# Decoding the first twelve weight blocks by way of PSUM, with their low parts made on GpSimd, in a fused attention and feed-forward kernel

## The chip, the cores and the metric

The kernel runs on one core of a Trainium2 chip. The metric is device time in microseconds (us) for one execution. In the profile PE is the matrix engine (PEld its weight loads), DVE is VectorE, ACT is ScalarE, POOL is GpSimd and SP is SyncE, which here only issues DMAs.

## The reference

A sliding-window attention with four sink tokens feeds a feed-forward block. There are 4 batches, 8 heads, 768 positions and a head size of 64. The feed-forward matrices arrive as 64-bit floats.

```python
scores = (q @ k.transpose(0, 1, 3, 2)) / np.sqrt(D)
keep = is_sink | ((rel >= 0) & (rel < window))       # n_sink = 4, window = 128
a = softmax(np.where(keep, scores, -1e9))
x = (a @ v).transpose(0, 2, 1, 3).reshape(3072, 512)
h = x @ w_in                                          # 512 x 2048
g = np.where(h >= 1, h, np.where(h <= -1, 0, (h + 1) ** 2 / 4))
out = g @ w_out                                       # 2048 x 512
```

## The kernel before

**The attention** is cut into 64 units of one batch, one head and 384 query rows. Units 0 to 15 take a short path (`NATIVE = 16`). A unit's scores are three PE steps (L239). For each, DVE adds the mask, takes the row's peak and moves the tile out of PSUM (L243), and ACT takes the exponential (L246). POOL adds a small constant to the three row sums (L251), DVE takes their reciprocals (L252), and one DVE row (L266) and two ACT rows (L264) scale the probabilities. PE transposes them (L324, L326), ACT copies them back (L327, L331), and PE multiplies them with the values (L367). ACT copies two heads' result to `xn` (L369). For every fourth part of the model dimension, ACT and DVE split `xn` into a high and a low part (L479, L480). Eight units make one chunk of 384 tokens; the program has eight chunks, called chunk 0 to 7 here.

**The feed-forward part** works on one chunk at a time, beside the attention of the next one. `stage1` (L439) multiplies into `h_ps`, ACT and DVE apply g and split it (L446 to L450; in the first chunk POOL makes the low part, L450), and `stage2` (L458) multiplies into `o_ps`, three PSUM banks of the pool `ps_o`.

**The weights** are 32 blocks of 128 x 512 numbers, 16 of `w_in` and 16 of `w_out` in turn (n = 0 to 31), each 512 KB of 64-bit floats. `weights(n)` issues the load of block n+3 at the latest (L167; blocks 0 to 7 on SP's queue, the others on ACT's) and decodes block n with `decode`. Three DVE instructions put a 32-bit float together out of the two 32-bit words: a shift with a mask (L153), the sign and top bits (L154), the low word's bits (L155). ACT rounds that to the matrix format, which is the high part (L156), and DVE subtracts it, which gives the low part (L157). The three results share one tile `o` of the pool `moe`, which has two buffers.

**The order.** PE's order is written out by hand: `spread` lays one list of steps evenly between those of another. The order on the other engines comes from a scheduler that places each instruction where it expects it to be ready. Blocks of weights can therefore stand earlier in DVE's row than their step. The lists are cut by two constants: the first `WFIRST` weight steps are spread over the attention of chunk 0, those up to `WMID` over the first half of chunk 0's feed-forward part, which runs beside the attention of chunk 1, and the last four over the next stage:

```python
prev = wsteps[:WFIRST]
        if c == 0:
            prev = spread(wsteps[WFIRST:WMID], moe_steps(rows[0], tail, x0, range(NJ0), part))
        elif c == 1:
            prev = spread(wsteps[WMID:], moe_steps(rows[1], tail), WLEAD)
```

Of the kernel before, what the change touches and what calls it, by code (L numbers as in the profile page):

```python
# [8 lines left out]
F32 = mybir.dt.float32  # L9
F32R = mybir.dt.float32r  # L10
I32 = mybir.dt.int32
U8 = mybir.dt.uint8
AF = mybir.ActivationFunctionType
ALU = mybir.AluOpType

B, H, S, D = 4, 8, 768, 64
DM, DFF = 512, 2048
P = 128
# [15 lines left out]


CHECK = range(34, 34 + 2 * NJ)
WFIRST = 6
WMID = 28
AHEAD = 3
SYNC = 8  # L40
# [12 lines left out]
def attn_ffn(ctx, tc, qk, vx, vs, par, w_in, w_out, out):  # L53
    nc = tc.nc
# [3 lines left out]
    moe = ctx.enter_context(tc.tile_pool(name="moe", bufs=2))  # L58
# [3 lines left out]
    ps_o = ctx.enter_context(tc.tile_pool(name="ps_o", bufs=3, space=bass.MemoryType.PSUM))  # L62
# [12 lines left out]
    low, high = par_f[:, :, 0], par_f[:, :, 1]  # L75
# [66 lines left out]
    w_i = [const.tile([P, 2, DM], F32R, name=f"wi{j}") for j in range(NJ)]  # L142
    w_o = [None] * NJ
# [4 lines left out]
    both = const.tile([P, 2 * P], I32, name="both")  # L148
    nc.gpsimd.memset(both, -1)

    def decode(t, w, words):
        low, x = words[:, :, 0], words[:, :, 1]
        nc.vector.tensor_scalar(w, x, 3, 0x3FFFFFFF, op0=ALU.logical_shift_left, op1=ALU.bitwise_and)  # L153
        nc.vector.scalar_tensor_tensor(w, x, -0x40000000, w, op0=ALU.bitwise_and, op1=ALU.bitwise_or)  # L154
        nc.vector.scalar_tensor_tensor(w, low, 29, w, op0=ALU.logical_shift_right, op1=ALU.bitwise_or)  # L155
        nc.scalar.copy(t[:, 0], w.bitcast(F32))  # L156
        nc.vector.tensor_tensor(t[:, 1], w.bitcast(F32), t[:, 0].bitcast(F32), op=ALU.subtract)  # L157

    top = {}

    def weights(n):
        def f():
            j, i = n // 2, n % 2
            for k in range(n, min(n + min(AHEAD, NJ - n // 2 - 1) + 1, 2 * NJ)):
                if k not in raw:
                    raw[k] = wpool.tile([P, 2 * DM], I32, name="w")
                    (nc.sync if k < SYNC else nc.scalar).dma_start(raw[k], (w_in, w_out)[k % 2][k // 2].bitcast(I32))  # L167
            words = raw[n].rearrange("p (c two) -> p c two", two=2)
            if i:
                w_o[j] = wpool.tile([P, 2, DM], F32R, name="w")  # L170
            decode((w_i, w_o)[i][j], moe.tile([P, DM], I32, name="o"), words)
        return f


# [307 lines left out]
    def moe_steps(row0, tail, x=None, js=range(NJ), part=None):  # L482


        if x is None:
            x = xpool.tile([P, 2, NCT, CT * P], F32R, name="x")
        o_ps, hs = [], {}
        steps = [(0.0, lambda ct=ct: split(x, ct)) for ct in range(NCT)] if js[0] == 0 else []
        second = tail[:]
        for n, j in enumerate(js):  # L490
            if n < LAG:
                steps += second[n * CT:(n + 1) * CT]
            steps += [(0.49, lambda j=j, ct=ct: stage1(x, j, ct, hs, row0)) for ct in range(NCT)]
            if n >= LAG:
                steps += [(0.65, lambda j=js[n - LAG], tt=tt: stage2(o_ps, hs, j, tt, row0, js, part)) for tt in range(CT)]
        tail[:] = [(0.65, lambda j=j, tt=tt: stage2(o_ps, hs, j, tt, row0, js, part)) for j in js[-LAG:]
                   for tt in range(CT)]
        return steps

    def spread(a, b, lead=1.0):  # L500

        wa, wb = (sum(w for w, _ in s) for s in (a, b))
        steps, n, da, db = [], 0, 0.0, 0.0
        for step in b:
            while n < len(a) and da * lead * wb <= db * wa:
                steps.append(a[n])
                da += a[n][0]
                n += 1
            steps.append(step)
            db += step[0]  # L510
        return steps + a[n:]
# [7 lines left out]
    rows = [b * S + t0 * P for b, t0 in chunks]  # L519
    prev = wsteps[:WFIRST]  # L520
    n0 = 0
    tail = []
    for c in range(len(chunks)):
# [5 lines left out]
# [3 lines that stand above are left out]
# [24 lines left out]
    ps = ps_a.tile([P, 512], F32, name="ps_a")  # L556
# [56 lines left out]
    with tc.If(other_v > 0):  # L613
        with tc.tile_pool(name="gen", bufs=1) as gen:

            for n in range(2 * NJ):
                words = gen.tile([P, DM, 2], I32, name="words")
                nc.sync.dma_start(words.rearrange("p c two -> p (c two)"), (w_in, w_out)[n % 2][n // 2].bitcast(I32))
                xf = words[:, :, 1].bitcast(F32)
                m = gen.tile([P, DM], F32, name="m")  # L620
                nc.vector.tensor_tensor(m, xf, xf, op=ALU.mult)
                nc.vector.scalar_tensor_tensor(xf, m, TINY2, xf, op0=ALU.is_ge, op1=ALU.mult)
                decode((w_i, w_o)[n % 2][n // 2], m.bitcast(I32), words)
            for t0 in (0, CT):
                keep = gen.tile([P, CT, S], F32, name="keep")
                kidx = gen.tile([P, S], I32, name="kidx")
                r = gen.tile([P, S], F32, name="r")
                for i in range(CT):
                    m = keep[:, i]
                    nc.gpsimd.iota(kidx, pattern=[[-1, S]], base=(t0 + i) * P, channel_multiplier=1)  # L630
                    nc.vector.tensor_copy(r, kidx)
                    nc.vector.tensor_scalar(m, r, w_f, None, op0=ALU.is_lt)
                    nc.vector.scalar_tensor_tensor(m, r, 0.0, m, op0=ALU.is_ge, op1=ALU.mult)
                    nc.gpsimd.iota(kidx, pattern=[[1, S]], base=0, channel_multiplier=0)
                    nc.vector.tensor_copy(r, kidx)
                    nc.vector.scalar_tensor_tensor(m, r, n_f, m, op0=ALU.is_lt, op1=ALU.max)
                    nc.vector.tensor_scalar(m, m, 0.125, None, op0=ALU.mult)
                for b in range(B):
                    for h in range(H):
                        general(gen, keep, b, h, t0)  # L640
                    tail = []
                    for _, f in moe_steps(b * S + t0 * P, tail) + tail:
                        f()
# [37 lines left out]
```

## Time and profile before

| what | value |
|---|---|
| median of 3 runs | 736.66 us (735.27 to 738.84) |
| the profiled execution | 737.31 us, span of its instructions 735.5 us |
| PE busy | 696.8 us, 95% of the span |
| DVE busy | 528.7 us, 72% |
| ACT busy | 507.0 us, 69% |
| POOL busy | 307.2 us, 42% |
| DMA | 77.79 MB, mean 106 GB/s |

The span is the time from the first to the last instruction of the program; about 1.8 us of the profiled execution lie outside it. A share over the whole span says little here: the first 100 us, in which the weights are decoded, look different from the rest, so the stages are read one by one.

### The profile page before, as it was taken

What the parts mean: (1) busy time and instruction counts of PE and PEld (TensorE: products, weight loads), DVE (VectorE), ACT (ScalarE), POOL (GpSimd) and SP (SyncE); (2) the same over time, 40 slices, a digit from 0 to 9 for tenths busy, and PEclk for the clock granted to TensorE, in tenths of its full rate; (3) what the DMA queues carried; (4) which work ended last, traced back from release to release, by engine and by line L of the source; (5) the groups of instructions that cost most, each with busy time, mean ns of one, the idle gap of its engine ahead of it and who ended that gap; (6) DMA issues with size and microseconds to landing.
All of it is one profiled execution on the core that took longest, in us unless ns stands there. A gap on an engine that the chain in (4) does not pass through costs nothing.

```text
span 735.5 us, 12356 instructions
## 1 busy us (share of the span) xinstructions
PE 696.8 (95%) x3841; PEld 615.7 (84%) x3841; DVE 528.7 (72%) x1396; ACT 507.0 (69%) x1313; POOL 307.2 (42%) x537
## 2 busy tenths in 40 slices
PE   5669889899999999999999999999999999999996
PEld 3337678789999999999979998899889999989995
DVE  8999996987655666568777887877887777742221
ACT  4888797776576665578767876778767776645342
POOL 3112166554346434236554555645666454500000
PEclk9989999999999999999999999999999999999998
DMA  8987543312131311134423542324334342101001
GB/s 268 327 268 255 170 115 96 99 46 54 42 100 45 100 40 58 34 119 128 124 81 117 156 121 85 116 73 156 124 114 119 103 131 85 66 2 44 0 1 47
DMA packets 48265, 77.79 MB, mean 106 GB/s; under 512 B 13632, under 2 KB 32064, under 8 KB 48192
## 3 DMA queue, kind: packets, MB, share of 16 engines
q1 hardware_dynamic: 44736, 64.34, 28.9%
q10 hardware_dynamic: 3456, 12.58, 4.8%
q8 instruction: 32, 0.52, 0.3%
q14 instruction: 41, 0.34, 0.2%
HBM read 69.83 MB, written 7.08 MB: 105 GB/s over the span
## 4 chain that ended last, share of the span: by engine, by line
PE 64%; DVE 17%; ACT 7%; DMA 7%; issue 2%; POOL 2%; SPq 0%; ACTq 0%; POOLq 0%; DVEq 0%
PE o_ps L458 28%; PE h_ps L439 27%; PE ps_a L402 4%; DMA w<-w_in 4%; PE ps_a L239 3%; ACT p L246 2%; DVE p L266 2%; DVE k_s L223 1%; DVE o L154 1%; PE ps_a L334 1%; DVE o L155 1%; DVE p L258 1%; DVE gl L450 1%; DVE p L243 1%; DVE o L153 1%
## 5 line engine op out<-in xcount | busy, mean ns | idle before, releaser
L439 PE MATMUL h_ps<-x,wi 128*128 128x384 f32 x1536 | 308.7, 340 | 0.4 <-DVE x L480 0.4
L439 PEld LDWEIGHTS h_ps<-x,wi 128*128 128x128 f32 x1536 | 263.5, 188 | 9.3 <-DVE x L480 0.7
L458 PE MATMUL o_ps<-w,gh 128*128 128x512 f32 x768 | 244.6, 399 | 0.0
L458 PE MATMUL o_ps<-w,gl 128*128 128x512 f32 x384 | 151.3, 394 | 0.0
L458 PEld LDWEIGHTS o_ps<-w,gh 128*128 128x128 f32 x768 | 135.2, 189 | 15.7 <-issue 0.3
L446 ACT ACTIVATE g<-h_ps,half 128x384 f32<-128x384 f32 x128 | 73.9, 578 | 69.7 <-PE h_ps L439 67.7
L448 DVE SCALAR_TENSOR_TENSOR g<-g,h_ps 128x384 f32<-128x384 f32 x128 | 70.2, 549 | 68.6 <-ACT g L447 68.0
L246 ACT ACTIVATE p<-p,peak 128x260 f32<-128x260 f32 (+1 forms) x192 | 93.9, 489 | 33.9 <-DVE peak L243 32.0
L225 POOL TENSOR_TENSOR q_l<-r,q_h 128x384 fp32r<-128x384 f32 x48 | 50.3, 1047 | 142.5 <-ACT q_h L224 141.6
L449 ACT CAST gh<-g 128x384 fp32r<-128x384 f32 x128 | 65.5, 512 | 56.9 <-DVE g L448 55.9
L243 DVE CUSTOM_DVE_ANT_0 p<-ps_a,m 128x260 f32<-128x260 f32 (+1 forms) x176 | 68.5, 398 | 31.8 <-PE ps_a L239 30.5
L239 PE MATMUL ps_a<-k_s,q_h 128*128 128x260 f32 (+1 forms) x240 | 71.2, 345 | 18.6 <-DMA k_s<-qk 6.1
L458 PEld LDWEIGHTS o_ps<-w,gl 128*128 128x128 f32 x384 | 72.3, 188 | 17.5
L450 DVE TENSOR_TENSOR gl<-g,gh 128x384 fp32r<-128x384 f32 x112 | 68.0, 607 | 24.5 <-ACT gh L449 23.6
L223 DVE TENSOR_TENSOR k_s<-k_r,k_s 64x524 fp32r<-64x524 f32 (+1 forms) x44 | 45.4, 1032 | 40.9 <-ACT k_s L221 40.9
L239 PEld LDWEIGHTS ps_a<-k_s,q_h 128*128 128x128 f32 x240 | 45.2, 203 | 33.3 <-issue 10.9
L447 ACT ACTIVATE g<-g 128x384 f32<-128x384 f32 x128 | 67.0, 523 | 2.7
L346 POOL TENSOR_SCALAR_AFFINE_SELECT pt<-pt 128x384 fp32r<-128x384 f32 (+1 forms) x96 | 50.8, 530 | 24.2 <-DVE pt L339 21.7
L266 DVE TENSOR_SCALAR p<-p,stat 128x132 f32<-128x132 f32 (+1 forms) x160 | 59.1, 418 | 0.3
L344 POOL TENSOR_SCALAR_AFFINE_SELECT pt<-pt 128x384 fp32r<-128x384 f32 (+1 forms) x96 | 52.5, 547 | 8.9 <-ACT pt L338 3.9
L251 POOL TENSOR_SCALAR stat<-stat 128x3 f32<-128x3 f32 x64 | 28.6, 447 | 62.2 <-ACT p L246 53.8
L402 PEld LDWEIGHTS ps_a<-pt,v_s 128*128 128x128 f32 x304 | 46.5, 189 | 2.0
(117 smaller groups left out, 955.3 us busy)
## 6 DMA issues: line engine op xcount, KB each, us to landing
r<-qk SPq DMA_DIRECT2D x48, 192.0 KB
k_r<-qk SPq DMA_DIRECT2D x32, 262.0 KB
again<-w_in SPq DMA_DIRECT2D x16, 512.0 KB
again<-w_out SPq DMA_DIRECT2D x16, 512.0 KB
w<-w_in ACTq DMA_DIRECT2D x12, 512.0 KB
w<-w_out ACTq DMA_DIRECT2D x12, 512.0 KB
out<-o SPq DMA_DIRECT2D x23, 256.0 KB
r<-vx SPq DMA_DIRECT2D x32, 128.0 KB
```

The source lines that it names most:

```text
L239: nc.tensor.matmul(ps[:, lo:260], lhsT=q[:, i * P:(i + 1) * P], rhs=k_s[:, c0:c0 + 260 - lo], start=(j == 0), stop=(j == len(qs) - 1))
L243: nc.vector.tensor_tensor_reduce(out=p[:, i, lo:260], in0=ps[:, lo:260], in1=m, scale=-0.0625 if units.index(u) < NATIVE else -0.125, scal ...
L246: nc.scalar.activation(p[:, i, lo:260], p[:, i, lo:260], AF.Exp, bias=peak_i, scale=-1.0, accum_out=stat[:, i:i + 1])
L266: (nc.gpsimd if eng == "p" else nc.vector).tensor_scalar(p[:, i, lo:260], p[:, i, lo:260], r, None, op0=ALU.mult)
L402: nc.tensor.matmul(z, lhsT=w, rhs=y, start=(n == 0), stop=(n == len(mms) - 1))
L439: nc.tensor.matmul(h_ps[:, :T], lhsT=w_i[j][:, w, ct * P:(ct + 1) * P], rhs=x[:, y, ct], start=(ct == 0 and n == 0), stop=(ct == NCT - 1 a ...
L446: nc.scalar.activation(g, h_ps[:, :T], AF.Relu, bias=half, scale=0.5)
L447: nc.scalar.activation(g, g, AF.Square)
L448: nc.vector.scalar_tensor_tensor(g, g, 1.0, h_ps[:, :T], op0=ALU.min, op1=ALU.max)
L449: nc.scalar.copy(gh, g)
L450: (nc.gpsimd if row0 == GL_POOL else nc.vector).tensor_tensor(gl, g, gh.bitcast(F32), op=ALU.subtract)
L458: nc.tensor.matmul(o_ps[tt], lhsT=gg[:, tt * P:(tt + 1) * P], rhs=w_o[j][:, w], start=(j == js[0] and n == 0), stop=(j == js[-1] and n == 2))
```

## The change

`WFIRST` goes from 6 to 12. For these first 12 blocks `decode` gets a PSUM tile of the pool `ps_o`. The first two DVE instructions write to it and the second and third read from it, so that each of the three has one SBUF tensor as input, the words, and from the second on one PSUM tensor. The third still writes `o` in SBUF. The low part of these blocks is subtracted by GpSimd instead of DVE. The other 20 blocks are decoded as before, and so is the copy in the branch at the end, which doesn't run with these inputs.

```diff
-WFIRST = 6
+WFIRST = 12
...
-    def decode(t, w, words):
+    def decode(t, w, words, ps=None):
         low, x = words[:, :, 0], words[:, :, 1]
-        nc.vector.tensor_scalar(w, x, 3, 0x3FFFFFFF, op0=ALU.logical_shift_left, op1=ALU.bitwise_and)
-        nc.vector.scalar_tensor_tensor(w, x, -0x40000000, w, op0=ALU.bitwise_and, op1=ALU.bitwise_or)
-        nc.vector.scalar_tensor_tensor(w, low, 29, w, op0=ALU.logical_shift_right, op1=ALU.bitwise_or)
+        y = w if ps is None else ps
+        nc.vector.tensor_scalar(y, x, 3, 0x3FFFFFFF, op0=ALU.logical_shift_left, op1=ALU.bitwise_and)
+        nc.vector.scalar_tensor_tensor(y, x, -0x40000000, y, op0=ALU.bitwise_and, op1=ALU.bitwise_or)
+        nc.vector.scalar_tensor_tensor(w, low, 29, y, op0=ALU.logical_shift_right, op1=ALU.bitwise_or)
         nc.scalar.copy(t[:, 0], w.bitcast(F32))
-        nc.vector.tensor_tensor(t[:, 1], w.bitcast(F32), t[:, 0].bitcast(F32), op=ALU.subtract)
+        (nc.vector if ps is None else nc.gpsimd).tensor_tensor(t[:, 1], w.bitcast(F32), t[:, 0].bitcast(F32), op=ALU.subtract)
...
-            decode((w_i, w_o)[i][j], moe.tile([P, DM], I32, name="o"), words)
+            decode((w_i, w_o)[i][j], moe.tile([P, DM], I32, name="o"), words,
+                   ps_o.tile([P, DM], F32, name="o_ps").bitcast(I32) if n < WFIRST else None)
```

In the changed file the lines of `decode` stand 3 lower (L153 to L157 become L156 to L160) and all that follows `weights` 4 lower (L243 becomes L247, L252 becomes L256, L266 becomes L270). The text below uses the numbers of before for both.

DVE's row of before, from the last rows of unit 3's scores (`m_106` is the mask of a unit's third part, `m_109` of its first) to the first part of unit 4's:

```order
L243 ISA p,peak<-ps_a,m_106 128x260
L243 ISA peak 128x1
L155 SCALAR_TENSOR_TENSOR o<-w,o 128x512
L153 TENSOR_SCALAR o<-w 128x512
L154 SCALAR_TENSOR_TENSOR o<-w,o 128x512
L252 RECIPROCAL stat<-stat 128x3
L155 SCALAR_TENSOR_TENSOR o<-w,o 128x512
L266 TENSOR_SCALAR p<-p,stat 128x128
L243 ISA p,peak<-ps_a,m_109 128x128
```

The same place in DVE's row of the change, from unit 3's reciprocals to the first part of unit 4's scores:

```order
L256 RECIPROCAL stat<-stat 128x3
L157 SCALAR_TENSOR_TENSOR o_ps<-w,o_ps 128x512
L270 TENSOR_SCALAR p<-p,stat 128x128
L156 TENSOR_SCALAR o_ps<-w 128x512
L158 SCALAR_TENSOR_TENSOR o<-w,o_ps 128x512
L157 SCALAR_TENSOR_TENSOR o_ps<-w,o_ps 128x512
L156 TENSOR_SCALAR o_ps<-w 128x512
L158 SCALAR_TENSOR_TENSOR o<-w,o_ps 128x512
L157 SCALAR_TENSOR_TENSOR o_ps<-w,o_ps 128x512
L158 SCALAR_TENSOR_TENSOR o<-w,o_ps 128x512
L247 ISA p,peak<-ps_a,m_109 128x128
```

More of the decoding now stands ahead of unit 4's scores: by then nine rows of L155 have gone by against six, and seven rows of decoding lie between unit 3's reciprocals and unit 4's scores against one.

POOL's row of before, from the constants at the start (`wi_151` is the `w_in` part of block 0, `wi_152` of block 2 and so on; `w` is a `w_out` part) over the first units' row sums:

```order
L113 MEMSET m1n 128x4
L251 TENSOR_SCALAR stat<-stat 128x3 x3
L298 TENSOR_TENSOR vsx_137<-vs_r,vsx_137 44x64
L251 TENSOR_SCALAR stat<-stat 128x3
L283 MEMSET v_s 128x128
```

The same place in POOL's row of the change:

```order
L113 MEMSET m1n 128x4
L255 TENSOR_SCALAR stat<-stat 128x3 x2
L160 TENSOR_TENSOR wi_151<-o,wi_151 128x512
L160 TENSOR_TENSOR w<-o,w 128x512
L160 TENSOR_TENSOR wi_152<-o,wi_152 128x512
L160 TENSOR_TENSOR w<-o,w 128x512
L255 TENSOR_SCALAR stat<-stat 128x3
L302 TENSOR_TENSOR vsx_137<-vs_r,vsx_137 44x64
L160 TENSOR_TENSOR wi_153<-o,wi_153 128x512
L255 TENSOR_SCALAR stat<-stat 128x3
```

Four low parts now stand ahead of the row sum of unit 2, and a fifth ahead of that of unit 3.

## Rows read from the trace of the kernel before

**Rows 1.** The page: busy tenths of PE and DVE in 40 slices.

```profile
PE   5669889899999999999999999999999999999996
...
DVE  8999996987655666568777887877887777742221
```

**Rows 2.** Stretches: length, then busy PE, PEld, DVE, ACT, POOL, clock, DMA, GB/s.

```profile
20.00:40.00 20.00, 13.53 (x78) 7.65 (x76) 19.44 (x61) 17.50 (x56) 2.28 (x8) 0.96 0.92 315
...
60.00:80.00 20.00, 19.39 (x115) 16.06 (x113) 19.93 (x52) 17.39 (x50) 5.43 (x7) 1.00 0.64 198
...
82.30:105.80 23.50, 21.83 (x126) 17.40 (x126) 22.41 (x53) 19.28 (x55) 9.78 (x11) 0.93 0.49 151
```

**Rows 3.** Timeline of DVE at 27 us: start, duration, instruction, [idle before it].

```profile
26.72 0.42 DVE L243 CUSTOM_DVE_ANT_0 p<-ps_a,m 128x260 f32<-128x260 f32 x1
...
27.06 0.42 DVE L153 TENSOR_SCALAR o<-w 128x512 int32<-128x512 int32 x1
27.40 0.54 DVE L480 TENSOR_TENSOR x<-xn,x 128x384 fp32r<-128x384 f32 x1
27.87 0.68 DVE L157 TENSOR_TENSOR w<-o,w 128x512 fp32r<-128x512 f32 x1
28.47 0.68 DVE L154 SCALAR_TENSOR_TENSOR o<-w,o 128x512 int32<-128x512 int32 x1
29.08 0.28 DVE L243 CUSTOM_DVE_ANT_0 p<-ps_a,m 128x128 f32<-128x128 f32 x1
29.28 0.08 DVE L243 DVE_READ_ACCUMULATOR2_ANT peak<- 128x1 f32 x1
```

**Rows 4.** Timeline of DVE at the reciprocals of unit 12.

```profile
80.65 0.16 DVE L252 RECIPROCAL stat<-stat 128x3 f32<-128x3 f32 x1
```

**Rows 5.** Timelines of ACT and PE behind it.

```profile
81.76 0.91 ACT L264 ACTIVATE p<-p,stat 128x260 f32<-128x260 f32 x2
...
82.33 0.86 PE L324 MATMUL ps_a<-ident,p 128*128 128x128 f32 x2 [2.38 <-ACT p L264]
```

**Rows 6.** PE's waits from 82.3 to 160 us: total us, times, longest.

```profile
PE ps_a L324 <- ACT p L264: 2.7, 2, 2.4
PE ps_a L239 <- DVE sk L341: 2.7, 2, 1.7
PE ps_a L239 <- DVE peak L243: 1.2, 2, 0.8
PE ps_a L239 <- ACT xn L369: 1.1, 1, 1.1
```

**Rows 7.** Timeline of POOL: tensor-tensor rows of 384 and of 192 elements.

```profile
69.13 1.00 POOL L450 TENSOR_TENSOR gl<-g,gh 128x384 fp32r<-128x384 f32 x1 [4.84 <-ACT gh L449]
...
72.24 1.50 POOL L450 TENSOR_TENSOR gl<-g,gh 128x384 fp32r<-128x384 f32 x1 [0.75 <-ACT gh L449]
...
93.72 1.34 POOL L225 TENSOR_TENSOR q_l<-r,q_h 128x384 fp32r<-128x384 f32 x1
...
95.78 1.25 POOL L450 TENSOR_TENSOR gl<-g,gh 128x384 fp32r<-128x384 f32 x1
...
110.06 0.59 POOL L293 TENSOR_TENSOR v_s<-r,v_s 128x192 fp32r<-128x192 f32 x1 [1.17 <-ACT v_s L292]
```

**Rows 8.** Timeline of DVE beside those rows of POOL.

```profile
69.21 1.20 DVE L153 TENSOR_SCALAR o<-w 128x512 int32<-128x512 int32 x1
...
72.79 1.04 DVE L266 TENSOR_SCALAR p<-p,stat 128x128 f32<-128x128 f32 x1
...
94.11 1.50 DVE L155 SCALAR_TENSOR_TENSOR o<-w,o 128x512 int32<-128x512 int32 x1
...
96.17 0.39 DVE L243 CUSTOM_DVE_ANT_0 p<-ps_a,m1n 128x260 f32<-128x260 f32 x1
```

**Rows 9.** DMA queue of ACT (q10: packets, MB, share): whole span.

```profile
q10 hardware_dynamic: 3456, 12.58, 4.8%
```

**Rows 10.** The same queue from 20 to 30 us.

```profile
q10 hardware_dynamic: 349, 1.30, 35.8%
```

## The prediction

> **What bounds the kernel now.** I looked at the slices of the page first. PE is short of work only in the first slices; from 160 us on it is busy in every one, so a microsecond gained or lost before that goes into the end time [rows 1]. The early part is therefore read by stretches. There DVE is full: 19.44 of 20 us from 20 to 40, 19.93 from 60 to 80 [rows 2]. PE has 13.53 us in the first of these, but 19.39 in the second, and 115 matmul rows there, 5.75 in a microsecond. From 82.3 to 105.8 it has 126, at that pace 21.9 of the 23.5 us [rows 2]. So up to some 60 us DVE alone sets the pace, and from there PE has only little room left.
>
> DVE works in order and hardly waits, so a row's time is that of all that stands ahead of it. What one row costs is the step from its start to the next start, not its duration, since neighbours overlap: L153 0.34 us, L157 0.60, L154 0.61 [rows 3]; I use 0.34 for L153 and 0.60 for L154, L155 and L157. A block costs DVE 2.14 us.
>
> The clearest place where PE waits for this queue is at unit 12's end: DVE's reciprocals (L252) start at 80.65, ACT scales the probabilities at 81.76, PE transposes them at 82.33 after 2.38 us of idling [rows 4, 5]. Behind it PE's waits up to 160 us come to 7.7 us, these 2.4 among them, which leaves 5.3, most of it on DVE [rows 6].
>
> **The change part by part.** *The low part leaves DVE:* 12 rows of 0.60, minus 7.2 us there.
>
> *The first instruction writes to PSUM.* No DVE row of before writes there. The lower bound is what it costs now, 0.34 for 512 numbers, the upper bound L154's 0.60 on the same tile. Rows that read PSUM are the nearest: L243 takes 0.34 to the next start for 260 numbers and 0.20 for 128 [rows 3], 1.06 ns a number, which at 512 gives 0.34 + 252 x 1.06 ns = 0.61. I take 0.60: 12 x 0.26 = 3.1 us back. The Trainium skill speaks against this edit at that point: "VectorE: DVE Perf Modes", section "Why PSUM operands drop a tier", says that the double rate of 32-bit tensor-scalar work needs both SBUF ports and that any PSUM operand ends it. By that rule the price is likewise the upper one; if only the row of L153 counted, it would be nothing and the sum 3.1 us less.
>
> The second and third instruction I leave at 0.60, the pace of one number a cycle that L243's slope has too.
>
> *The order.* This is the largest part. I counted the rows of L153, L154, L155 and L157 ahead of three places, in both orders; the attention's rows ahead of them are the same but for a row or two.
> - Chunk 0's last split (the fourth L480), which the feed-forward part needs: before 18, 18, 18, 17, after 22, 21, 21, 8. Before 18 x 0.34 + 53 x 0.60 = 37.9 us; after 12 x 0.60 + 10 x 0.34 + 50 x 0.60 = 40.6. **2.7 us later.**
> - Unit 12's reciprocals: before 23, 23, 23, 21 (48.0 us), after 27, 27, 26, 14 (12 x 0.60 + 15 x 0.34 + 67 x 0.60 = 52.5). **4.5 us later.**
> - The last split of chunk 1 (the eighth L480): 29 of each before (62.1 us), after 29, 29, 29, 17 (58.0). **4.1 us earlier.**
>
> The saving is thus paid out only at the end of the stretch; in its middle, where PE waits, the changed queue is late.
>
> *GpSimd's low parts.* A POOL subtraction takes 1.00 us for 384 numbers undisturbed and 0.59 for 192 [rows 7], so 1.00 + 128 x 2.1 ns = 1.27 for 512, 15.3 us for twelve. POOL is busy for only 2.28 of 20 us there [rows 2], so it has the time. But beside such rows some of DVE's are held up: L153 takes 1.20 instead of 0.42, L266 1.04 where another row of 128 numbers takes 0.28 [rows 3], L155 1.50 instead of 0.68, each ending about when a POOL row does, while L243 at 96.17 with its tensor in PSUM is not touched, 0.39 [rows 7, 8]. A meeting costs up to 0.8 us, 0.4 in the mean. The twelve low parts lie between 14 and 40 us or so, 15.3 of 26 us, a share of 0.59. DVE rows of the kinds held up stand there 13 times by the order: six L266, two L480 and five of blocks 12 and 13. 13 x 0.59 x 0.4 = **3.1 us**, bounds 0 and 13 x 0.8 = 10.4.
>
> *Waits for words and buffers.* The loads from block 8 on stand in ACT's row behind the same roundings as before, while DVE comes to the blocks sooner. The queue moves 3456 packets for 24 blocks, 144 each [rows 9], and 349 between 20 and 30 us [rows 10]: blocks 8 and 9 are there by 30, block 10 not. By my count DVE comes to block 9 at 30.2 (before 35.3), to block 10 at 31.8 (38.5). The margin of about 5 us is used up, hardly overdrawn: **0.5 us**, bounds 0 and 3. The roundings of twelve blocks are ACT's as before (17.50 of 20 us busy [rows 2]). POOL's row sums stand behind low parts now, so DVE's reciprocals may wait for them; that is the third rival.
>
> *What PE gets back.* At unit 12 PE is late by 4.5 + 3.1 + 0.5 = 8.1 us. Behind that it comes later than before while DVE's queue is shorter, so what it waited for is ready: the 5.3 us of waits are taken back. Sum: +2.8 us on the profiled 737.31 (its span of 735.5 and some 1.8 around it), 740.1. That execution lay 0.65 us above the median, so I forecast **739.5 us** against 736.66.
>
> **The rivals.**
> 1. *The end of the stretch decides* (faster). If PE can swallow its backlog, what counts is the third place, 4.1 us earlier. With the port met half as often (1.5) and 0.5 for words, and with 2.0 us fewer hold-ups late in the stretch, since 10 rows of decoding are left there instead of 26: -4.1, so 733.2, 732.5 beside the median. For it speaks that PE's busy time includes matmuls that wait; against it that PE does 5.4 rows a microsecond there, close to its pace of 5.75 [rows 2]. It decides if PE needs under 17 us for that work. If the first instruction also kept 0.34, it would be 3.1 less.
> 2. *The port is met in full* (slower): 13 x 0.59 x 0.8 = 6.1 instead of 3.1, as low parts follow each other without gaps: +5.8, 742.5. The four low parts in a row in POOL's order speak for it.
> 3. *GpSimd paces the decoding* (slower). The tile `o` has two buffers and is now freed by POOL, so block n+2's third instruction waits for the low part of block n, behind ACT's rounding. Rounding and subtraction and some 0.5 us of queueing make 0.6 + 1.27 + 0.5 = 2.4 us; DVE has about 3 us from one use of a buffer to its next, so it fits until ACT comes more than 0.6 us late. ACT is nearly full and waits for DVE's scores itself. At 0.6 us for each of ten blocks: +8.8, 745.5.
>
> **How the numbers follow.** About 0.5%, 3.7 us, is what a measurement of this kernel can tell from no change. Forecast 0.46, with a range of its own from 736 to 742; rival 1 0.20; rival 2 0.16; rival 3 0.18. A tenth of the forecast's case lies above 740.3. So faster 0.20, same 0.42, slower 0.38. The range goes from 732, near rival 1, to 746, near rival 3.
>
> **What would show it.** L156 writing `o_ps` steps on by 0.60, not 0.34. POOL gets twelve rows of about 1.3 us before 45 us, and L266 and L480 of the first units show durations near 1 us. The fourth L480 starts some 3 to 6 us later than before, unit 12's reciprocals 5 to 9 us after 80.65, and PE's wait there grows. From 90 us on PE waits for DVE less. The prediction is wrong if L156 keeps 0.34, if DVE idles in the first 40 us (rival 3), or if PE catches up before 105 us.

## The result and the profile after

The change makes the kernel slower by 0.9%: 743.43 us in the median of 7 runs (741.07 to 744.46) against 736.66 (734.61 to 738.84, 7 runs), a ratio of 1.009 with a 95% interval of 1.0067 to 1.0113. The profiled execution took 743.43 us with a span of 741.7, 6.2 more than before.

Where the time goes is seen by the same instruction in both traces (start in us; lines of the changed file in this table; PE's order is the same in both kernels but for 62 of 3841 places):

| place | before | after | shift | forecast |
|---|---|---|---|---|
| chunk 0's first split (first L484) | 27.40 | 35.92 | +8.5 | |
| its last split (fourth L484) | 62.36 | 68.64 | +6.3 | 2.7 and up to 3.6 for port and words |
| unit 12's reciprocals (L256) | 80.65 | 88.20 | +7.5 | +8.1 |
| sixth block of g in the feed-forward part (L452) | 103.79 | 106.82 | +3.0 | +7.7 |
| tenth block of g | 133.05 | 141.56 | +8.5 | +6.2 |
| 16th to 48th block of g | 163.90 to 319.48 | 172.44 to 328.00 | +8.5 | +2.8 |
| end | 735.5 | 741.7 | +6.2 | +2.8 |

Behind unit 12 the forecast column takes off before's waits of PE as they come: 0.36 us at 97 us, 1.5 at 105 to 108, 3.6 at 137 to 148. So two losses, not one: the forecast one, and one more between 107 and 142 us. The +3.0 at the sixth g is a place in DVE's row; PE's own rows are later there, as is shown further down.

The slices of the page after: PE's are fuller in the third and sixth, emptier in the fourth and eighth, DVE's nearly as full as they were [rows 1], and PE's granted clock dips from the second to the fourth slice and in the eighth.

```profile
PE   5678899799999999999999999999999999999996
...
DVE  8899956797754576658788788878878777842221
...
PEclk9778999899999999999999999999999999999999
```

The stretches [rows 2]: DVE is no longer full from 20 to 40 us (17.68 for 19.44), GpSimd's time rose from 2.28 to 10.52, and PE's clock is 0.68 where it was 0.96. The last row is new.

```profile
20.00:40.00 20.00, 13.11 (x51) 7.60 (x50) 17.68 (x50) 14.56 (x46) 10.52 (x14) 0.68 0.92 318
82.30:105.80 23.50, 21.31 (x129) 17.28 (x129) 18.16 (x50) 20.28 (x61) 8.30 (x12) 1.00 0.43 125
140.00:160.00 20.00, 16.64 (x79) 14.45 (x80) 19.69 (x50) 11.03 (x31) 8.90 (x16) 0.83 0.22 66
```

Before, that last stretch was PE's:

```profile
140.00:160.00 20.00, 18.96 (x108) 16.81 (x108) 17.65 (x48) 14.12 (x40) 10.48 (x18) 1.00 0.24 70
```

DVE's timeline after:

```profile
25.11 0.69 DVE L156 TENSOR_SCALAR o_ps<-w 128x512 int32<-128x512 int32 x1
25.71 0.68 DVE L158 SCALAR_TENSOR_TENSOR o<-w,o_ps 128x512 int32<-128x512 int32 x1
...
40.96 1.24 DVE L270 TENSOR_SCALAR p<-p,stat 128x128 f32<-128x128 f32 x1
42.16 1.48 DVE L156 TENSOR_SCALAR o<-w 128x512 int32<-128x512 int32 x1
...
88.20 0.18 DVE L256 RECIPROCAL stat<-stat 128x3 f32<-128x3 f32 x1
...
135.23 0.43 DVE L156 TENSOR_SCALAR o<-w 128x512 int32<-128x512 int32 x1 [0.59 <-DMA part<-o]
...
139.75 0.43 DVE L156 TENSOR_SCALAR o<-w 128x512 int32<-128x512 int32 x1 [1.35 <-DMA part<-o]
...
141.56 0.55 DVE L452 SCALAR_TENSOR_TENSOR g<-g,h_ps 128x384 f32<-128x384 f32 x1
```

L156 into PSUM steps on by 0.60 (25.11 to 25.71) where L153 took 0.34 [rows 3]. The two rows at 41 and 42 us, written to SBUF, last 1.24 and 1.48 and end 0.08 and 0.28 us after GpSimd's last two low parts:

```profile
40.85 1.27 POOL L160 TENSOR_TENSOR wi<-o,wi 128x512 fp32r<-128x512 f32 x1 [0.21 <-ACT wi L159]
42.09 1.27 POOL L160 TENSOR_TENSOR w<-o,w 128x512 fp32r<-128x512 f32 x1
```

PE's timeline after: the wait at unit 12 shrank from 2.38 [rows 5] to 1.16, one of 1.03 us for the values of a unit is new at 115 us, and one of 3.18 us stands at 142 us.

```profile
89.67 0.73 PE L328 MATMUL ps_a<-ident,p 128*128 128x128 f32 x2 [1.16 <-ACT p L268]
...
114.87 0.64 PE L338 MATMUL ps_a<-ident,p 128*128 128x128 f32 x3 [1.03 <-ACT v_s L296]
...
142.16 1.44 PE L443 MATMUL h_ps<-x,wi 128*128 128x384 f32 x6 [3.18 <-DVE g L452]
...
145.85 0.56 PE L243 MATMUL ps_a<-k_s,q_h 128*128 128x260 f32 x1 [0.86 <-DVE sk L345]
```

The wait at 142 us is followed back to the stores of chunk 0's partial sums. Its feed-forward part is cut in two; at the end of the first half ACT copies three PSUM tiles to tiles `o`, SP stores them to `part`, and the last four weight blocks are decoded next, in the same two buffers of `o`. SP's queue before and after (`x3` with 3.34 us is a group of three):

```profile
125.48 1.15 SPq L465 DMA_DIRECT2D part<-o  x2
...
128.22 0.32 SPq L465 DMA_DIRECT2D part<-o  x1
```

```profile
132.27 3.34 SPq L469 DMA_DIRECT2D part<-o  x3
```

Before, DVE began the first of these blocks at 128.42 without a wait. After, its rows of L156 at 135.23 and 139.75 wait 0.59 and 1.35 us for the stores (rows above), 6.8 and 7.8 us later than before; L452, which PE waits for, stands behind them at 141.56, 8.5 later. Its input from ACT is there at 138.36 (the last row of the ACT timeline below); of the 3.2 us from then on, 1.35 are the second wait for the stores and the rest are rows of DVE ahead of it. Of the 6.8 us, 5 are those by which PE is already late at 125 us. The other 2 us arise at ACT: PE has the ninth block's h ready at 123.52 before and at 128.53 after, and ACT starts its g at 123.56 and at 130.63. Before, the cast of the next unit's values (L292) stood between the copies:

```profile
124.60 0.57 ACT L464 COPY o<-o_ps 128x512 f32<-128x512 f32 x1
125.44 0.35 ACT L292 CAST v_s<-r 128x192 fp32r<-128x192 f32 x1 [0.28 <-DMA r<-vx]
```

After, it stands ahead of that block's g and the copies, and waits for its load:

```profile
130.25 0.35 ACT L296 CAST v_s<-r 128x192 fp32r<-128x192 f32 x1 [1.10 <-DMA r<-vx]
130.63 0.58 ACT L450 ACTIVATE g<-h_ps,half 128x384 f32<-128x384 f32 x1
...
131.68 1.05 ACT L468 COPY o<-o_ps 128x512 f32<-128x512 f32 x2
...
137.82 0.54 ACT L451 ACTIVATE g<-g 128x384 f32<-128x384 f32 x1
```

### The profile page after: what moved, and what is told of

The parts are those of the page before. It is cut to its first block, busy times and chain, and to the rows that moved or that the text cites. A ratio compares the mean times of both kernels' runs of the same rounds, so it can differ in the third digit from the quotient of the medians.

```text
span 741.7 us, 12358 instructions
## 1 busy us (share of the span) xinstructions
PE 702.5 (95%) x3841; PEld 621.0 (84%) x3841; DVE 523.5 (71%) x1384; ACT 507.3 (68%) x1313; POOL 316.5 (43%) x549
## 4 chain that ended last, share of the span: by engine, by line
PE 62%; DVE 16%; ACT 8%; DMA 7%; issue 3%; POOL 2%; SPq 0%; ACTq 0%; POOLq 0%; DVEq 0%
PE o_ps L462 27%; PE h_ps L443 26%; PE ps_a L406 4%; PE ps_a L243 3%; ACT p L250 2%; DMA w<-w_out 2%; DVE p L270 2%; PE ps_a L338 1%; DVE k_s L227 1%; DVE o L158 1%; DVE gl L454 1%; DVE p L247 1%; DMA again<-w_out 1%; DVE p L262 1%; DVE g L452 1%
## 5 line engine op out<-in xcount | busy, mean ns | idle before, releaser
L462 PEld LDWEIGHTS o_ps<-w,gh 128*128 128x128 f32 x768 | 135.4, 189 | 15.8 <-issue 0.3
L452 DVE SCALAR_TENSOR_TENSOR g<-g,h_ps 128x384 f32<-128x384 f32 x128 | 70.2, 549 | 68.9 <-ACT g L451 68.3
L229 POOL TENSOR_TENSOR q_l<-r,q_h 128x384 fp32r<-128x384 f32 x48 | 48.8, 1017 | 151.3 <-ACT q_h L228 143.1
L247 DVE CUSTOM_DVE_ANT_0 p<-ps_a,m 128x260 f32<-128x260 f32 (+1 forms) x176 | 68.3, 399 | 33.1 <-PE ps_a L243 32.0
L243 PE MATMUL ps_a<-k_s,q_h 128*128 128x260 f32 (+1 forms) x240 | 71.4, 347 | 14.1 <-DMA k_s<-qk 5.3
L243 PEld LDWEIGHTS ps_a<-k_s,q_h 128*128 128x128 f32 x240 | 46.0, 208 | 27.3 <-issue 10.8
L270 DVE TENSOR_SCALAR p<-p,stat 128x132 f32<-128x132 f32 (+1 forms) x160 | 58.9, 417 | 0.5
L255 POOL TENSOR_SCALAR stat<-stat 128x3 f32<-128x3 f32 x64 | 26.6, 415 | 53.7 <-ACT p L250 45.0
```

What stands on the lines that cost most here:

```text
L243: nc.tensor.matmul(ps[:, lo:260], lhsT=q[:, i * P:(i + 1) * P], rhs=k_s[:, c0:c0 + 260 - lo], start=(j == 0), stop=(j == len(qs) - 1))
L247: nc.vector.tensor_tensor_reduce(out=p[:, i, lo:260], in0=ps[:, lo:260], in1=m, scale=-0.0625 if units.index(u) < NATIVE else -0.125, scal ...
L270: (nc.gpsimd if eng == "p" else nc.vector).tensor_scalar(p[:, i, lo:260], p[:, i, lo:260], r, None, op0=ALU.mult)
L452: nc.vector.scalar_tensor_tensor(g, g, 1.0, h_ps[:, :T], op0=ALU.min, op1=ALU.max)
L462: nc.tensor.matmul(o_ps[tt], lhsT=gg[:, tt * P:(tt + 1) * P], rhs=w_o[j][:, w], start=(j == js[0] and n == 0), stop=(j == js[-1] and n == 2))
```

## The experiments

A ratio is against runs of the kernel before on the same chip (736.70 us for the first four kernels, 736.72 for the next four, 737.57 and 736.84 for the last two pairs); its 95% interval stands behind it (a ratio can differ from the quotient of the two medians by up to 0.001). Shifts are those of the first table: us later than in the trace of before, each from one profiled execution, which lies up to 2.0 us from its kernel's median (path for 6 blocks 1.9, path for 12 2.0 and before with 5 ahead 2.0 above).

### The parts of the change apart

Before with the order's constant alone:

```diff
-WFIRST = 6
+WFIRST = 12
```

> WFIRST is 12, the decoding is that of before. Theory A (DVE's order is to blame: blocks stand ahead of the scores that PE waits for): by the rows counted in its order, chunk 0's last split is 4.2 us later than before, unit 12's reciprocals 5.9 us later, chunk 1's last split not earlier; with 1 to 3 us of waits for words and little taken back the time is 5 to 9 us above before. Rival B (the new decoding is to blame, by the PSUM price, the port and GpSimd): without it the order costs nothing, within 2 us of before.

The change with all low parts on DVE:

```diff
-        (nc.vector if ps is None else nc.gpsimd).tensor_tensor(t[:, 1], ...)
+        nc.vector.tensor_tensor(t[:, 1], ...)
```

> As the change, but the low parts stay on DVE. Theory A: the counted rows put unit 12's reciprocals 8.4 us after those of before and the last split of chunk 1 3.1 us after, so it is slower than the change: 8 to 13 us above before. Rival B, with GpSimd as the cause (port and the buffers of o): faster than the change, at most 4 us above before.

The change without PSUM, the low parts still on GpSimd:

```diff
-        y = w if ps is None else ps
+        y = w
```

> As the change, but the three decoding rows stay in SBUF. Theory A: the counted rows put unit 12's reciprocals 2.3 us before those of before and chunk 1's last split 7.2 us before; with two SBUF inputs the decoding rows now meet the twelve low parts on GpSimd, which gives back 3 to 8 us up to 45 us, and words cost up to 3: 0 to 7 us above before, below the change. Rival (meetings are as rare as in the change, 2 us): 2 to 4 us below before. Second rival (the PSUM way is what keeps DVE going): slower than the change.

The change with the partial sums stored from ACT's queue, so that they don't stand in SP's:

```diff
-                nc.sync.dma_start(part[tt], o)
+                nc.scalar.dma_start(part[tt], o)
```

> The change, with the partial sums' stores issued by ACT instead of SP. Theory C (of the change's loss, about 5 us arise between 106 and 150 us, where block 30's first decoding row waits for a buffer of o that a store frees, which stands in SP's queue behind loads): 3 to 5 us faster than the change, 738.5 to 740.5. Rival (that wait only shows what DVE and PE owe from before): within 1 us of the change.

| kernel | median us | ratio | fourth split | unit 12 | sixth g | tenth g | end of span |
|---|---|---|---|---|---|---|---|
| the change | 743.43 | 1.009 [1.0067, 1.0113] | +6.3 | +7.5 | +3.0 | +8.5 | +6.2 |
| WFIRST = 12 alone | 740.95 | 1.0059 [1.0037, 1.0081] | +5.3 | +6.7 | +3.4 | +6.1 | +4.0 |
| low parts on DVE | 744.53 | 1.0098 [1.0072, 1.0123] | +5.8 | +7.8 | +5.3 | +9.2 | +7.4 |
| no PSUM | 746.10 | 1.0126 [1.01, 1.0152] | +10.5 | +10.6 | +8.3 | +11.1 | +8.7 |
| stores on ACT's queue | 742.50 | 1.0071 [1.0046, 1.0097] | +5.4 | +6.6 | +2.1 | +5.0 | +5.9 |

The order alone costs 4.3 us of the 6.8 (theory A said 5 to 9) and makes most of the lateness at the fourth split and at unit 12. Taking twelve subtractions from DVE is worth 1.1 us in the end, less than the two intervals can tell. Moving the stores off SP's queue changed little: the tenth g came earlier, but by the 16th the shift was +7.6 again, so the theory that SP's queue is at fault fell. In that trace DVE waits for the stores for 0.81 us instead of 1.94, and PE waits less at the tenth g (0.84) but for 2.63 us at 143.30 and 1.80 at 154.51, both for DVE.

Without PSUM the kernel is the slowest of the four, as the second rival said (theory A had it faster than the change), and its trace says why. Rows of DVE from 9 to 60 us (busy us, mean ns), first without PSUM, then the change:

```profile
L158 DVE SCALAR_TENSOR_TENSOR o<-w,o 128x512 int32<-128x512 int32 x16 | 14.5, 907 | 0.1
L157 DVE SCALAR_TENSOR_TENSOR o<-w,o 128x512 int32<-128x512 int32 x16 | 13.8, 860 | 0.2
```

```profile
L156 DVE TENSOR_SCALAR o_ps<-w 128x512 int32<-128x512 int32 x12 | 8.3, 688 | 3.0 <-DMA w<-w_out 2.2 <-DMA w<-w_in 0.8
L157 DVE SCALAR_TENSOR_TENSOR o_ps<-w,o_ps 128x512 int32<-128x512 int32 x12 | 8.2, 683 | 0.0
L158 DVE SCALAR_TENSOR_TENSOR o<-w,o_ps 128x512 int32<-128x512 int32 x12 | 8.1, 678 | 0.1
```

Twelve rows of DVE last 1.1 to 1.7 us there, one beside each of GpSimd's twelve low parts; above their usual 0.28, 0.43, 0.55 and 0.68 us that is 11.1 us in all, 0.92 for one. In the change two rows are held up, 0.96 and 1.05. The rows with one operand in PSUM keep 0.68. The Trainium skill states this rule ("SBUF — State Buffer", section "Who interferes with whom": a VectorE instruction with at most one SBUF input, outside the two-port modes, does not contend with GpSimd), and these two traces agree with it.

### The path at six blocks, earlier loads, and the last four blocks

The change with the path, and its order, for six blocks:

```diff
-WFIRST = 12
+WFIRST = 6
```

> The change with WFIRST back at 6, so that only the first six blocks go by way of PSUM and GpSimd and the order of before is nearly kept (counted on DVE's row: the fourth split +0.1 us, unit 12's reciprocals +0.7). Theory A (the order that WFIRST = 12 brings makes most of the loss, the new path by itself little): 735.5 to 738.5 us, within 0.25% of before, and unit 12's reciprocals within 2 us of before's 80.65. Rival B (the path is what costs, by its PSUM steps, its waits for words and its meetings at the port): about half of the change's 6.8 us, 739.5 to 741 us.

The change with earlier loads of the words:

```diff
-AHEAD = 3
+AHEAD = 5
```

> The change with AHEAD = 5, so that each block's words are asked for two blocks earlier. Theory W (the 3.0 us in which DVE waits for words are on the path and stay lost): those waits gone, unit 12's reciprocals 3 to 6 us earlier than the change's 88.20, the end 2 to 4 us faster than the change, 739.5 to 741.5. Rival (PE takes such a gain back by 107 us and the loss between 120 and 150 us comes again whole): within 1 us of the change, 742.5 to 744.5.

The change, and then before, with all blocks decoded ahead of the partial sums:

```diff
-WMID = 28
+WMID = 32
```

> The change with WMID = 32, so that the last four blocks too are decoded beside the first half of chunk 0's feed-forward part and nothing is decoded between 125 and 150 us, where DVE's row stood twice for a buffer of o behind the stores of the partial sums. Theory D (that stretch's decoding makes the second loss, 3.0 us at 107 us to 8.5 us at 142 us): the wait of 3.18 us at 142.16 us is gone, the shift against before at g 16 is 0 to 3 us, the end 4 to 7 us faster than the change, 736.5 to 739.5. Rival (the four blocks cost before the eighth split what they cost behind it; counted on DVE's row that split comes 6.4 us later): within 1.5 us of the change.

> The kernel before with WMID = 32 alone. Theory D: before has PE waits of 1.68, 0.85 and 1.04 us in 135 to 150 us that go, against an eighth split that is counted 6.4 us later, of which PE can take back what it waits between 103 and 115 us: within 2 us of before, 734.5 to 738.5. Rival (DVE sets the pace up to the eighth split, and the four blocks are paid there in full): 740 to 743.

| kernel | median us | ratio | fourth split | unit 12 | sixth g | eighth g | 16th g | end of span |
|---|---|---|---|---|---|---|---|---|
| path for 6 blocks | 738.35 | 1.0013 [0.9995, 1.0032] | +2.6 | +2.6 | +0.7 | +0.6 | +3.9 | +3.1 |
| change, 5 ahead | 739.56 | 1.0043 [1.0017, 1.007] | +4.9 | +3.3 | -0.1 | +0.8 | +3.4 | +1.7 |
| change, WMID = 32 | 738.97 | 1.0037 [1.0023, 1.005] | +5.6 | +5.3 | +7.8 | +8.7 | +2.7 | +3.1 |
| before, WMID = 32 | 740.39 | 1.0048 [1.003, 1.0067] | -0.3 | +0.3 | +1.4 | +8.0 | +2.5 | +2.5 |

For six blocks the path costs nothing that can be measured (theory A's range; unit 12's reciprocals came 2.6 us late in the one trace, where it allowed 2).

With five blocks ahead the time is theory W's, but not its mechanism. DVE's waits for words fall from 3.0 us to 0.7, but it now waits 1.4 us for GpSimd, 0.9 of them for low parts, so only 0.9 us are gone. The first split comes 0.9 us earlier than the change's, unit 7's reciprocals 0.8 later (52.83 against 52.05). The gain appears at unit 12, where DVE's order has 26 blocks begun ahead of the reciprocals instead of 27. What DVE waits for from 9 to 60 us (us in total, times, longest), in the change and with five ahead:

```profile
DVE o_ps L156 <- DMA w<-w_out: 2.2, 2, 1.2
DVE o_ps L156 <- DMA w<-w_in: 0.8, 1, 0.8
```

```profile
DVE o L158 <- POOL w L160: 0.5, 1, 0.5
DVE stat L256 <- POOL stat L255: 0.5, 1, 0.5
DVE o_ps L156 <- DMA w<-w_in: 0.4, 1, 0.4
DVE o L158 <- POOL wi L160: 0.4, 1, 0.4
DVE o_ps L156 <- DMA w<-w_out: 0.3, 1, 0.3
```

WMID = 32 shows that the loss at 142 us needs the decoding there. With no decoding behind 125 us PE has no wait there (140 to 160 us, to be read against the rows of before and after above):

```profile
140.00:160.00 20.00, 20.00 (x118) 18.40 (x117) 16.43 (x47) 14.46 (x40) 10.78 (x20) 1.00 0.21 56
```

Between the eighth and the 16th g the shift falls by 6.0 us, where the change's grows by 3.5; 3.6 of the 6.0 are waits that the kernel before itself has in this stretch. In the kernel before, the same edit moves it by as much (8.0 to 2.5), and there the price ahead of it, four blocks more in front of the eighth split, is greater: the end is 3.7 us slower, the rival's range and not theory D's.

### Controls and versions that might beat both

Before with `AHEAD = 5`; then the change with `AHEAD = 5` and `WMID = 32`:

> The kernel before with AHEAD = 5 alone, as a control of the change with the same edit, which came out 3.9 us faster than the change. Theory W (the change gained by words that come in time, which before hardly waits for: 0.2 us): within 1.5 us of before, 735.5 to 738. Rival (earlier loads help whatever the decoding, by the order that they bring): 2 us or more faster than before, under 735.

> The change with AHEAD = 5 and WMID = 32 together, which alone made it 3.9 and 4.5 us faster. Theory W with D (two separate losses, one ahead of 90 us and one between 125 and 150 us): 4 to 8 us faster than the change, 735.5 to 739.5, at the best no slower than before. Rival (both give back the same microseconds, since PE makes up before 107 us only what the stretch leaves it): no faster than either alone, 739 to 741.

The path for all twelve blocks in the order of WFIRST = 6:

```diff
-WFIRST = 12
+WFIRST = 6
+NPS = 12
...
-  if n < WFIRST else None)
+  if n < NPS else None)
```

> The change's path for all twelve blocks with WFIRST back at 6, the counterpart of WFIRST = 12 alone. Blocks 6 to 11 then take their PSUM banks in the stretch in which chunk 0's feed-forward part holds three banks of the same pool; in DVE's row only 11 blocks stand ahead of the fourth split and 15 ahead of unit 12's reciprocals, against 18 and 23 before. Theory A (the path is cheap, the order is what costs): 736 to 740. Theory P (the path needs the order: decoding falls behind, and PE waits for weights between 60 and 130 us): 745 to 790, with waits of PE for a weight tile that no kernel so far shows.

The change with `WFIRST = 6` and `WMID = 32`:

> The new path for the first six blocks (WFIRST = 6) with WMID = 32, as a version that might beat both kernels. Theory D (the decoding behind 125 us is a loss of its own that every order but that of before pays with 3 to 5 us): 1 to 3 us faster than the same without WMID = 32 (738.35), 735.5 to 737.5. Rival (as in the kernel before, where WMID = 32 cost 3.7 us: the stretch up to the eighth split pays in full): 739.5 to 742.

| kernel | median us | ratio | fourth split | unit 12 | sixth g | tenth g | end of span |
|---|---|---|---|---|---|---|---|
| before, 5 ahead | 742.61 | 1.0074 [1.0046, 1.0101] | +3.9 | +5.5 | +6.2 | +5.9 | +7.3 |
| change, 5 ahead and WMID = 32 | 740.38 | 1.0032 [1.0008, 1.0055] | +5.5 | +5.4 | +2.9 | +6.7 | +4.5 |
| path for 12, WFIRST = 6 | 748.16 | 1.0155 [1.011, 1.02] | -3.6 | -4.1 | -3.7 | +15.8 | +12.9 |
| path for 6, WMID = 32 | 741.70 | 1.0064 [1.0035, 1.0092] | +2.3 | +4.3 | +3.6 | +7.9 | +5.0 |

The control missed on both sides: earlier loads make the kernel before 5 us slower. The words of blocks 4 and 5 are asked for at 5.24 and 6.67 us, ahead of a unit's keys on SP's queue, and PE waits for these for 2.63 us where it waited for 0.30. PE's timeline with five ahead, then of before:

```profile
17.47 2.50 PE L239 MATMUL ps_a<-k_s,q_h 128*128 128x128 f32 x6 [2.63 <-DMA k_s<-qk]
```

```profile
14.58 2.72 PE L239 MATMUL ps_a<-k_s,q_h 128*128 128x128 f32 x6 [0.30 <-DMA k_s<-qk]
```

So AHEAD is not a knob for words alone. The change with both edits is no faster than with either (the rival's reading), and with the path at six blocks WMID = 32 costs 3.4 us (the rival again). No version tried beats the kernel before.

The path for twelve blocks in the old order is the sharpest of them. It is 4 us early at 60 to 100 us, because the twelfth block's first row comes at 64.12 us, where it came at 41.30; DVE meanwhile waits for scores and for row sums, from 20 to 70 us:

```profile
DVE stat L257 <- POOL stat L256: 6.6, 6, 1.5
DVE p L248 <- PE ps_a L244: 5.7, 7, 2.2
```

The decoding left undone is paid behind 105 us, in the attention's and g's rows behind it: PE's waits there are nearly all for DVE, the longest 2.85 us at 128.32, none for a weight tile, so the time is in theory P's range but came by another way than it said.

## Why the prediction was right in direction and too small

**DVE sets the pace early, PE passes a shift on:** right. The shift of 8.5 us stands unchanged from 164 to 328 us. It is not quite passed on to the end: 2.3 us come back between 350 and 580, where the kernel before waited for DVE for 1.43 us at 369.52 and the changed one for 0.27.

**The first instruction's price:** right at 0.60 a step, the upper bound; the rule of the Trainium skill named there ("VectorE: DVE Perf Modes", section "Why PSUM operands drop a tier") agrees with it.

**GpSimd's low parts:** each took 1.27 to 1.30 us, as worked out. The port cost 2.0 us, not 3.1, and by another count: two meetings met in full, not 7.7 at 0.4. What I took as a mean per meeting was wrong; a meeting costs about 1 us or nothing, and the decoding rows with a PSUM operand have none. Of the 13 rows that I had counted as exposed, one L270 and one row of block 12 were held up. I also left out that before has hold-ups of its own up to unit 12, three of 0.77, 0.76 and 0.81 us; the change has three too (0.96, 1.05, 0.81), so the net price is 0.5 us. And the row of L155 in [rows 8] ended 0.55 us after GpSimd's, not with it.

**Words and buffers:** DVE waits 3.0 us, the upper bound, not 0.5; before waited for 0.8 us up to unit 12, so 2.2 us more. What they cost by themselves is not shown: five blocks ahead took 2.3 us of them away and put 1.4 us of waits for GpSimd in their place.

**The order:** right, and the largest term. Counted in the same way, WFIRST = 12 alone gives +4.3 at the fourth split and +5.8 at unit 12; measured +5.3 and +6.7. With all terms unit 12 was to be 8.1 late and was 7.5. That it came so near is in part luck: with the net prices the sum is 4.5 + 0.5 + 2.2 = 7.2, the port 2.6 us less than I said and the words 1.7 more.

**What PE gets back:** this is the step that failed. I took the 5.3 us out of all waits up to 160 us [rows 6], those at 137 to 148 us too, with the reason that DVE's queue is shorter behind unit 12. Instead PE waits 6.1 us from 90 to 165 us:

```profile
PE h_ps L443 <- DVE g L452: 3.2, 1, 3.2
PE ps_a L243 <- DVE sk L345: 1.2, 2, 0.9
PE ps_a L338 <- ACT v_s L296: 1.0, 1, 1.0
PE ps_a L243 <- ACT spn L335: 0.5, 1, 0.5
PE ps_a L339 <- DVE sk L276: 0.2, 1, 0.2
```

What PE did get back is read from its own rows, one and the same in both traces. At unit 12's transposes it is 7.3 us late (89.67 against 82.33), at the products with the values behind them (L367) 5.8, without a wait between. That gain of 1.6 us goes with the clock, a term that I had put at nothing: before, the granted clock fell behind the wait of 2.38 us, and 12 rows took 3.60 us where the change had 20 in 3.20. Before, then after:

```profile
82.30:86.00 3.70, 3.60 (x12) 2.72 (x12) 3.70 (x8) 2.33 (x8) 0.23 (x1) 0.56 0.32 117
```

```profile
82.30:86.00 3.70, 3.20 (x20) 2.54 (x19) 3.67 (x11) 2.34 (x9) 0.03 (x1) 1.00 0.73 240
```

Another 2.0 us, most of them before's waits of 0.36, 1.13 and 0.39, bring PE to 3.7 late at 113 us. Then it loses again: 1.2 at 115 us, where it waits for a unit's values, 0.4 up to 139, and 3.2 at 142 us. The 3.6 us of before's waits from 137 us on give nothing back, since PE waits 1.2 us there itself and its matmuls take 2.4 us more at the lower clock (see the last section).

So the +3.0 at the sixth g does not show that PE took back what I said. PE's own row there is 5.7 late, before and after:

```profile
98.56 0.71 PE L458 MATMUL o_ps<-w,gh 128*128 128x512 f32 x2
```

```profile
104.22 0.62 PE L462 MATMUL o_ps<-w,gh 128*128 128x512 f32 x2
```

Before, that row of g stood in a full queue (DVE busy for 4.83 of 5 us from 100 to 105); after, DVE is busy for 2.20 of 5.

DVE's queue is not shorter in the whole stretch: the last four blocks are decoded from 125 us on in both kernels. They need the buffers of `o` that the partial sums are stored from; with a later and tighter row of copies and stores the first two started 6.8 and 7.8 us late. That PE's loss at 142 us needs the decoding in this stretch is shown (without it PE has no wait there). Whether the buffers' wait or the crowding of DVE's rows behind it decides is open. For the crowding speaks that with the stores on ACT's queue less waiting for buffers only moved PE's waits to 143 and 154 us; a third buffer was not tried.

The sum with the measured terms, on PE's rows: 7.3 late at unit 12, 3.6 taken back by 113 us, 4.8 lost again by 142 us, 2.3 regained later: +6.2.

**The signs.** L156's step, GpSimd's rows and unit 12's place came as I said. But PE's wait at unit 12 shrank where I said that it grows, only one L270 (L266 before) and no L484 (L480) was held up, PE waited no less for DVE from 90 us on (4.6 us against 3.9), and DVE idled in the first 40 us, which I had named as a sign of being wrong: 3.0 us, for words and not, as in rival 3, for GpSimd.

**The rivals.** Rival 1 fell: the eighth split came 6.1 us late, not early. Rival 2 gave nearly the measured time, 742.5, by a mechanism that took 2.0 us, not 6.1. Rival 3 fell: up to 60 us DVE never waits for a buffer of `o` held by GpSimd in the change.

## What to carry to other kernels

Count what a change of order puts ahead of the rows that the bottleneck waits for; here that gave the early loss of WFIRST = 12 alone within 1.0 us, while twelve subtractions taken from the full engine gave no gain that could be measured. Take back only waits that stand before the next place where the same engine has work of the old size, and read what PE takes back on PE's own rows: at the sixth g DVE's row said 3.0 us and PE's 5.7. An early saving is worth nothing if the work behind it is only put off: twelve blocks in the old order were 4 us ahead at 100 us and 13 behind at the end.

## What was not expected of the hardware

Keeping one operand of VectorE's rows in PSUM cuts the hold-ups beside GpSimd's twelve low parts from twelve (11.1 us) to two (2.0 us). By the medians that is worth 2.7 us here, and GpSimd's help 1.1.

PE's granted clock was at the lower of its two levels (1.2 of 2.4 GHz), 0.50, from 145 to 150 us behind the wait of 3.18 us, with 13 matmul rows in 4.15 us where the next stretch has 31 in 5.00. Before, the clock there was 1.00, though PE had waited for 1.68 and 0.85 us shortly ahead. At unit 12 it was the other way: 0.56 behind before's wait of 2.38 us, 1.00 behind the change's of 1.16. After, by stretches of 5 us:

```profile
135.00:140.00 5.00, 3.98 (x23) 3.27 (x21) 3.32 (x5) 4.95 (x14) 1.93 (x3) 1.00 0.33 101
140.00:145.00 5.00, 2.83 (x11) 2.32 (x11) 4.97 (x12) 1.72 (x6) 2.40 (x5) 0.82 0.10 25
145.00:150.00 5.00, 4.15 (x13) 3.68 (x14) 4.84 (x15) 3.34 (x9) 1.55 (x2) 0.50 0.42 136
150.00:155.00 5.00, 5.00 (x31) 4.62 (x30) 4.94 (x11) 3.59 (x12) 3.35 (x6) 1.00 0.22 60
```

Without its waits PE took 13.60 us for the 60 rows from 142.16 us on, 11.20 before. At the end this cost nothing that shows: DVE is full in these stretches, PE still waits 0.34 us for it at 156.96, and PE's shift is 8.5 us at both places.
